# Moving SBUF-only products and casts to GpSimd, and pairing the fifth q tiles, in a fused linear-attention and gated feed-forward kernel

## The chip, the cores and the metric

The kernel runs on one core of a Trainium2 chip. Five engines work side by side: TensorE (PE; its weight loads are listed as PEld), VectorE (DVE), ScalarE (ACT), GpSimd (POOL) and SyncE (SP, which issues most of the DMAs). The metric is the device time of one execution in microseconds; less is better.

## The reference

Linear attention with cosine weighting for 8 batches of 8 heads, 576 tokens and 64 features, and behind it a feed-forward layer over all 4608 tokens:

```python
def phi(x, c, s):                       # c, s: cos and sin of (pi/2) * pos / S
    r = np.maximum(x, 0.0)
    return np.concatenate([r * c, r * s], axis=-1)
q_p, k_p = phi(q, cos_w, sin_w), phi(k, cos_w, sin_w)
kv = np.einsum('bhsf,bhsd->bhfd', k_p, v)
z = np.sum(k_p, axis=2)
num = np.einsum('bhsf,bhfd->bhsd', q_p, kv)
den = np.einsum('bhsf,bhf->bhs', q_p, z)[..., None] + 1e-06
x = (num / den)                         # to (4608, 512)
h = x @ w_in                            # 512 -> 2048
g = h * np.cos(h)
out = g @ w_out                         # 2048 -> 512
```

## The kernel before, in words

**Tiles of tokens.** A batch has 576 tokens: four tiles of 128 and 64 tokens left over, which form a fifth tile that is half full. A batch's tokens lie in two interleaved halves of the partitions: `load` brings five tiles of one half's 64 partitions (every second one) and four tiles of the other's; which half has five depends on whether the batch is even or odd. The fifth tiles of two batches together make one tile of 128 tokens, so there are nine chunks of 512 tokens for the feed-forward layer: chunks 0 to 7 are the batches' four full tiles, and chunk 8 gathers the four paired fifth tiles.

**Attention of a batch** (`first_attention`, `second_attention`, `attention`). `prep` (L364 on ACT, L365 on DVE) applies ReLU and the cosine or sine weight to a 128x512 tile of k or q, SBUF to SBUF, fp32 to fp16. `cast_v` (L378 ACT, L379 DVE) casts v to fp16; only for batches 0 and 1 may it also be put on POOL, and the order in use puts none there. `kv` (L391) makes the k-v products. A q tile is transposed either by PE (`q_pe`, L420, with a copy out of PSUM) or by DMA (`q_dma`, L428, on SP's queue). `num` (L450) multiplies the transposed q tile by the k-v products; DVE divides (L474, L476); `x_pe` (L496) or `x_dma` (L504) transposes the result into `xT` or, for fifth tiles, `xR`.

**A fifth q tile before the change.** The q tile of each batch is prepared and transposed on its own, with zeros in the half of the partitions that belongs to the other batch (the memsets at L962 clear them once); it goes to `qT4_0` or `qT4_1`. For an odd batch `num` then sums two products per head, the earlier batch's and its own. For batch 0 a function of its own, `late_q0`, does this with PE during layer 1 of chunk 0.

**Layer 1 of a chunk** (`layer1`). For chunks 0 and 1 blocks of two columns by 256 tokens (L542). From chunk 2 on a column block is either plain (`layer1_plain`, L582: four matmuls of 512 columns, then a gate), or four blocks together are done by a seven-product scheme (`layer1_fast`, L685: 28 matmuls of 256 columns). `FAST1` says how many of a chunk's four groups are of the second kind; chunk 2 has none. The scheme needs sums of weights (`w_in_sums`, into `WS`), sums of the tokens' tile (`layer1_sums`, into `XS`), and copies and additions out of PSUM into `Z3` (L318, L319, L698).

**Gates.** `gate` is h * cos(h) of one PSUM bank: ACT makes the cosine (L514, into `ch`), DVE multiplies (L519; one operand in PSUM, the other in SBUF). In a seven-product group half of the results lie in SBUF (`uz`); `out2` makes one cosine over 1024 elements (L707) and one product of 1024 elements with both operands in SBUF. This product, like all of `sums`, is a DVE instruction at L323. A page line `L323 ... gT<-Z,ch` is such a product; `S<-gT`, `gT<-gT`, `XS<-xT`, `WS<-w_in_sb` and `T<-w_out_sb` are the fp16 sums.

**Layer 2** (`layer2_plain` for chunk 0, L784; else `layer2`, L849) is done by the same seven-product scheme over the whole chunk, with DVE sums of the gated values ahead of it, and its results go by L318, L319 and L863 into `ost` and by DMA (L745) to the output.

**The order.** All instructions are first put down as steps (`Plan.add`) with their possible engines. A long table `KEYS` gives for each step its place (the number divided by ten, in hundredths of a microsecond of the plan's own time) and, as its last digit, which of the possible engines takes it (0 where there is only one). The steps are then issued in the order of their places, so each engine's queue has a fixed order; synchronization is by what the steps read and write. Chunk c's layer 1 overlaps layer 2 of chunk c-1 and the attention of the batches behind it.

Of the kernel before, what the change touches and what calls it, by code (L numbers as in the profile page):

```python
# [12 lines left out]
F32 = mybir.dt.float32  # L13
# [180 lines left out]
def kernel(  # L194
# [9 lines left out]
    nc = tc.nc  # L204
    B, H, S, D = q.shape
    Dm, Dff = moe_w_in.shape
    P = 128
# [886 lines left out]
```

## Time and profile before

| | |
|---|---|
| time, median of 3 runs | 281.59 us (280.68 to 282.78) |
| the profiled execution | 280.85 us, of it 279.0 us from the first to the last instruction |
| granted TensorE clock | 0.999 |
| busy PE / PEld / DVE / ACT / POOL | 269.2 / 217.3 / 251.4 / 218.9 / 8.3 us |
| the DVE products with both operands in SBUF, 128x1024 | 20, of some 1.22 us |
| preps on ACT / DVE | 104 of some 0.73 us / 56 of some 0.48 us |
| v casts on ACT / DVE / POOL | 20 / 18 / 0 |

All durations are of one execution, the profiled one. Busy time is the time in which an engine has at least one instruction under way; instructions of one engine overlap by some hundredths of a microsecond, so that preps of 0.48 us start every 0.40 us. PE's matmuls overlap far more: a row's mean is the time until a matmul's last result, and the spacing of matmuls is what adds up.

### The profile page before, as it was taken

How to read it: one execution, taken by the hardware profiler on the slowest of the kernel's cores; microseconds unless marked ns; L12 is line 12 of the kernel's file. 1: busy time of each engine (PE TensorE's matmuls, PEld its weight loads, DVE VectorE, ACT ScalarE, POOL GpSimd, SP SyncE). 2: the span in 40 equal slices, each digit the busy share in tenths (PEclk: the TensorE clock that was granted, in tenths of full speed). 3: DMA queues.
4: the chain of work that ended last, by engine and by line, in shares of the span. 5: the costliest groups of instructions: out<-in, count | busy, mean ns of one | idle time of the engine just before them, and what ended most of it. 6: DMA issues, size and time to landing. Idle time of an engine off the chain costs nothing.

```text
span 279.0 us, 6853 instructions
## 1 busy us (share of the span) xinstructions
PE 269.2 (96%) x2715; PEld 217.3 (78%) x2715; DVE 251.4 (90%) x449; ACT 218.9 (78%) x401; POOL 8.3 (3%) x21
## 2 busy tenths in 40 slices
PE   7779999999999999999999999999999999999994
PEld 2458767678766677789879887998788888888883
DVE  2977798999999999999999999999999999998872
ACT  2856698899999999999999999984684686777210
POOL 1430020000000000000000000000000000000000
PEclk9999999999999999999999999999999999999999
DMA  6999999999999999999999999737210400200324
GB/s 208 315 201 232 281 312 282 309 218 172 328 269 253 210 288 247 310 235 230 245 264 195 346 277 265 154 58 205 39 39 4 188 2 0 78 0 2 151 78 150
DMA packets 77599, 53.30 MB, mean 191 GB/s; under 512 B 46080, under 2 KB 75264, under 8 KB 77568
## 3 DMA queue, kind: packets, MB, share of 16 engines
q1 hardware_dynamic: 72608, 48.12, 67.7%
q0 software_dynamic: 4224, 4.19, 9.3%
q10 hardware_dynamic: 736, 0.57, 0.6%
q8 instruction: 21, 0.34, 0.5%
q14 instruction: 10, 0.08, 0.1%
HBM read 36.74 MB, written 9.44 MB: 166 GB/s over the span
## 4 chain that ended last, share of the span: by engine, by line
PE 85%; DMA 5%; ACT 4%; DVE 3%; issue 2%; ACTq 0%
PE M L849 33%; PE M L685 15%; PE M L542 8%; PE M L582 7%; PE TR L685 6%; PE M L784 4%; PE ATT L450 3%; DMA qT<-KQ 3%; PE ATT L391 3%; DMA qm<-in_q_dram 2%; ACT KQ L364 2%; PE TR L582 1%; ACT ch L514 1%; PE M L420 1%; DVE KQ L365 1%
## 5 line engine op out<-in xcount | busy, mean ns | idle before, releaser
L514 ACT ACTIVATE ch<-M 128x512 f32<-128x512 f32 x90 | 53.9, 603 | 14.0 <-PE M L685 6.8
L849 PEld LDWEIGHTS <-gT 128*128 128x128 f16 x560 | 54.1, 98 | 8.2
L519 DVE TENSOR_TENSOR gT<-M,ch 128x512 f16<-128x512 f32 x84 | 55.9, 685 | 4.5 <-ACT ch L514 4.0
L849 PE MATMUL M<-w_out_sb,gT 128*128 128x256 f16 x448 | 56.4, 273 | 0.0
L364 ACT ACTIVATE KQ<-km,CS 128x512 f16<-128x512 f32 x56 | 38.9, 732 | 0.5 <-DMA km<-in_k_dram 0.5
L364 ACT ACTIVATE KQ<-qm,CS 128x512 f16<-128x512 f32 x48 | 33.5, 728 | 4.4 <-DMA qm<-in_q_dram 4.2
L685 PEld LDWEIGHTS <-w_in_sb 128*128 128x128 f16 x320 | 31.0, 98 | 4.6 <-issue 0.2
L849 PE MATMUL M<-T,S 128*128 128x256 f16 x256 | 31.5, 273 | 0.0
L318 ACT ACTIVATE ost<-M 128x512 f32<-128x512 f32 x32 | 19.2, 600 | 15.0 <-PE M L849 9.5
L542 PE MATMUL M<-xT,w_in_sb 128*128 128x256 f16 x256 | 30.1, 272 | 0.6 <-DVE gT L519 0.5
L542 PEld LDWEIGHTS <-w_in_sb 128*128 128x128 f16 x256 | 24.6, 98 | 4.8 <-issue 1.2
L582 PE MATMUL M<-xT,w_in_sb 128*128 128x512 f16 x112 | 27.9, 379 | 0.0
L849 PEld LDWEIGHTS <-S 128*128 128x128 f16 x256 | 24.9, 98 | 3.4
L476 DVE TENSOR_TENSOR x<-ATT,rec 128x512 f16<-128x512 f32 x32 | 22.1, 692 | 2.5
L685 PEld LDWEIGHTS <-WS 128*128 128x128 f16 x216 | 20.6, 98 | 2.6
L582 PEld LDWEIGHTS <-w_in_sb 128*128 128x128 f16 x128 | 11.9, 98 | 9.2
L365 DVE TENSOR_SCALAR KQ<-qm,CS 128x512 f16<-128x512 f32 x32 | 14.2, 479 | 4.8 <-DMA qm<-in_q_dram 4.8
L450 PEld LDWEIGHTS <-qT 128*128 128x128 f16 x320 | 14.7, 98 | 4.4 <-issue 1.4
L323 DVE TENSOR_TENSOR S<-gT 128x2048 f16<-128x2048 f16 (+1 forms) x16 | 17.2, 1083 | 0.0
L450 PE MATMUL ATT<-kvz,qT 128*128 128x65 f16 x288 | 15.3, 194 | 0.9 <-DVE kvz L406 0.4
L323 DVE TENSOR_TENSOR gT<-Z,ch 128x1024 f16<-128x1024 f32 x13 | 15.9, 1219 | 0.3
L698 DVE TENSOR_TENSOR Z<-M,Z 128x512 f32<-128x512 f32 x22 | 14.9, 686 | 0.9 <-PE M L685 0.5
(138 smaller groups left out, 448.6 us busy)
## 6 DMA issues: line engine op xcount, KB each, us to landing
out_dram<-ost SPq DMA_DIRECT2D x33, 256.0 KB, 2.7
qm<-in_q_dram SPq DMA_DIRECT2D x8, 640.0 KB, 5.7
km<-in_k_dram SPq DMA_DIRECT2D x8, 640.0 KB, 6.5
qm<-in_q_dram SPq DMA_DIRECT2D x8, 512.0 KB, 6.0
km<-in_k_dram SPq DMA_DIRECT2D x8, 512.0 KB, 6.5
vm<-in_v_dram SPq DMA_DIRECT2D x6, 640.0 KB, 6.8
vm<-in_v_dram SPq DMA_DIRECT2D x6, 512.0 KB, 6.6
w_in_sb<-in_moe_w_in_dram POOLq DMA_DIRECT2D x4, 512.0 KB, 8.6
```

Source lines behind the costliest of these rows:

```text
L318: "ACT": lambda: nc.scalar.activation(out=out_, in_=in_, func=AF.Copy),
L323: return lambda: q.tensor_tensor(out=out_, in0=in0, in1=in1, op=op)
L364: fn = {"ACT": lambda: nc.scalar.activation(out=out_, in_=in_, func=AF.Relu, scale=sc), "DVE": lambda: nc.vector.tensor_scalar(out=out_, i ...
L365: "DVE": lambda: nc.vector.tensor_scalar(out=out_, in0=in_, scalar1=0.0, scalar2=sc, op0=ALU.max, op1=ALU.mult)}
L450: nc.tensor.matmul(bank[hb][:, hh * D1:(hh + 1) * D1], lhsT=a[:, h, :], rhs=z[:, h, :], start=(i == 0), stop=(i == len(parts) - 1))
L476: nc.vector.tensor_tensor(out=split(x16[n][:, hs, :], k), in0=A[:, :, :, 0:D], in1=split(rec[n][:, hs], k).unsqueeze(3).broadcast_to((P, k ...
L514: act(0.5, due, lambda: nc.scalar.activation(out=ch[c], in_=bank, func=AF.Sin, bias=math.pi / 2.0, scale=1.0), [key], [("ch", c)])
L519: dve(0.61, due, lambda: nc.vector.tensor_tensor(out=dst, in0=a, in1=b, op=ALU.mult), [key, ("ch", c), *rd], dkeys)
L542: nc.tensor.matmul(M1[m][:, jj * 2 * P:(jj + 1) * 2 * P], lhsT=w_in_sb[:, cc, j * P:(j + 1) * P], rhs=X[:, cc, ts], start=(jj == 0 and cc ...
L582: nc.tensor.matmul(M, lhsT=w_in_sb[:, cc, j * P:(j + 1) * P], rhs=X[:, cc, :], start=(cc == 0), stop=(cc == NCT - 1))
L685: nc.tensor.matmul(bank[0][:, j * TH:(j + 1) * TH], lhsT=a(cc, j), rhs=b[:, cc, :], start=(first and j == 0 and cc == 0), stop=(last and j ...
L849: nc.tensor.matmul(bank[0][:, tt * MH:(tt + 1) * MH], lhsT=a[:, j, tt * P:(tt + 1) * P], rhs=b[:, j, :], start=(first and (apart or tt == ...
```

## The change

- `sums` gets an option for POOL, and `out2` uses it: the 1024-element product may go to POOL. `cast_v` may go to POOL for every batch. The order table is new throughout. By its digits, 17 of the 21 products and 21 of the 38 v casts are on POOL; the rest of the work is also divided anew between ACT and DVE.
- Chunk 2 has one seven-product group instead of four plain column blocks; its weight sums come before layer 1 of chunk 2.
- The fifth q tiles of two batches are prepared and transposed together, when the odd batch's turn comes: both batches' loads leave their rows in the two halves of one raw tile. `CS` gets a column with both batches' weights. `late_q0` and the memset of q are gone, `qT4` is one buffer. `num` takes for the fifth tile every second column of `qT4` (64 columns) against one batch's k-v products, and writes 64 rows of PSUM for each batch. The stores of chunk 8 read 64 neighbouring partitions instead of every second one.

```diff
 KEYS = (
...
 )
-    cs_np = np.zeros((P, 2, 2, NT + 1), dtype=np.float32)
+    cs_np = np.zeros((P, 2, 2, NT + 2), dtype=np.float32)
...
-            cs_np[n::2, n, g, :] = w[:S5].reshape(R, NT + 1)
+            cs_np[n::2, n, g, :NT + 1] = w[:S5].reshape(R, NT + 1)
+            cs_np[n::2, :, g, NT + 1] = w[NT:S5:NT + 1, None]
...
-    qT4 = [sb(f"qT4_{n}", [P, H, P]) for n in range(2)]
+    qT4 = sb("qT4", [P, H, P])
...
-    VCAST, VCAST_01 = ("DVE", "ACT"), ("DVE", "ACT", "POOL")
+    VCAST = ("DVE", "ACT", "POOL")
...
-    def sums(due, n, out_, in0, in1, op, rd, wr, lazy=None, rate=0.523e-3):
+    def sums(due, n, out_, in0, in1, op, rd, wr, lazy=None, rate=0.523e-3, pool=None):
         def go(q):
             return lambda: q.tensor_tensor(out=out_, in0=in0, in1=in1, op=op)
-        either(due, {"DVE": 0.07 + n * rate, }, {"DVE": go(nc.vector)}, rd, wr,
-               lazy=lazy)
+        cost = {"DVE": 0.07 + n * rate}
+        if pool:
+            cost["POOL"] = pool
+        either(due, cost, {"DVE": go(nc.vector), "POOL": go(nc.gpsimd)}, rd, wr, lazy=lazy, port=False, hint=1)
...
-        sc = CS[:, b % 2, g, t:t + 1]
+        sc = CS[:, b % 2, g, t + (nm == "q" and t == NT):][:, 0:1]
...
-        either(due, {e: cost[e] for e in (VCAST if b > 1 else VCAST_01)}, fn, rd, wr)
+        either(due, {e: cost[e] for e in VCAST}, fn, rd, wr, port=False)
...
-        parts = [(qdst(b, t)[0], kvz[b % 2])]
+        a = qdst(b, t)[0]
         rd = [qdst(b, t)[1]] + [("kvz", b % 2, i) for i in range(2)]
         if t == NT:
-            parts.insert(0, (qT4[1 - b % 2], kvz[1 - b % 2]))
-            rd += [("qT4", 1 - b % 2)] + [("kvz", 1 - b % 2, i) for i in range(2)]
+            rd += [("kvz", 1 - b % 2, i) for i in range(2)]
...
-                for i, (a, z) in enumerate(parts):
+                for n2 in range(2) if t == NT else [None]:
+                    rows_, cols, z = (slice(0, P), slice(0, P), kvz[b % 2]) if n2 is None else (
+                        slice(n2 * R, (n2 + 1) * R), slice(n2, P, 2), kvz[n2])
                     nc.tensor.matmul(
-                        bank[hb][:, hh * D1:(hh + 1) * D1], lhsT=a[:, h, :], rhs=z[:, h, :],
-                        start=(i == 0), stop=(i == len(parts) - 1))
+                        bank[hb][rows_, hh * D1:(hh + 1) * D1], lhsT=a[:, h, cols], rhs=z[:, h, :],
+                        start=True, stop=True)
...
-    FAST1 = {3: 3, 4: 3, 5: 3, 6: 3, 7: 4, 8: 4}
+    FAST1 = {2: 1, 3: 3, 4: 3, 5: 3, 6: 3, 7: 4, 8: 4}
...
-                 rate=1.045e-3)
+                 rate=1.045e-3, pool=2.6)
...
-        for i, nm in enumerate("qkv"):
+        for i, nm in enumerate("kv"):
...
-        for t in range(NT + 1):
+        for t in range(NT + b % 2):
             due = T + 8 + 1.2 * t
...
-    def late_q0():
-        for g in range(2):
-            prep(0, "q", NT, g, "DVE", 24, after=[("g", 0, 0, 0)])
-        q_pe(0, NT, TR, ("TR", 0), "ACT", 25)
-
     first_attention()
     layer1(0)
-    late_q0()
```

More of the change, by code (lines that the diff above doesn't have):

```diff
@@ L237, in sb @@
         return pool.tile(shape, dt, name=name)
-    CS = sb("CS", [P, 2, 2, NT + 1], F32)
+    CS = sb("CS", [P, 2, 2, NT + 2], F32)
     IDENT = sb("IDENT", [P, P])
@@ L411, in qdst @@
     def qdst(b, t):
-        return (qT[t], ("qT", t)) if t < NT else (qT4[b % 2], ("qT4", b % 2))
+        return (qT[t], ("qT", t)) if t < NT else (qT4, "qT4")
     def q_pe(b, t, bank, key, eng, due):
@@ L448, in mm @@
                 h = hb * HB + hh
-                for i, (a, z) in enumerate(parts):
+                for n2 in range(2) if t == NT else [None]:
+                    rows_, cols, z = (slice(0, P), slice(0, P), kvz[b % 2]) if n2 is None else (
+                        slice(n2 * R, (n2 + 1) * R), slice(n2, P, 2), kvz[n2])
                     nc.tensor.matmul(
-                        bank[hb][:, hh * D1:(hh + 1) * D1], lhsT=a[:, h, :], rhs=z[:, h, :],
-                        start=(i == 0), stop=(i == len(parts) - 1))
+                        bank[hb][rows_, hh * D1:(hh + 1) * D1], lhsT=a[:, h, cols], rhs=z[:, h, :],
+                        start=True, stop=True)
         full.update((key, False) for key in keys)
         for hb in range(2):
-            pe(HB * len(parts), MMA, due, lambda hb=hb: mm(hb), rd, [keys[hb]])
+            pe(HB * (1 + (t == NT)), MMA, due, lambda hb=hb: mm(hb), rd, [keys[hb]])
         if pair is None:
@@ L761, in store @@
             dst = out.rearrange("(i n s) m -> n i s m", n=2, s=S)[n][2 * h + i0:2 * h + 2, 0:S5, f]
-            put(due, dst.rearrange("i (p t) m -> p t i m", t=NT + 1)[:, NT], blocks(O, n)[:, i0:, f],
+            put(due, dst.rearrange("i (p t) m -> p t i m", t=NT + 1)[:, NT], O[n * R:(n + 1) * R, i0:, f],
                 keys, *((nc.scalar, "ACT") if n else (nc.sync, "SP")), nb=kb / (1 + i0))
@@ L767, in store_tile @@
             dst = out.rearrange("(i n s) m -> n i s m", n=2, s=S)[n][2 + i, 0:S5, 0:MH]
-            put(due, dst.rearrange("(p t) m -> p t m", t=NT + 1)[:, NT], blocks(ost[o], n)[:, i, 0:MH],
+            put(due, dst.rearrange("(p t) m -> p t m", t=NT + 1)[:, NT], ost[o][n * R:(n + 1) * R, i, 0:MH],
                 [("ost", o, 0, i)], *((nc.scalar, "ACT") if n else (nc.sync, "SP")), nb=65.5)
```

241 rows, old and new, of the table KEYS are left out of this document.

## The prediction

> **What bounds the kernel now.** I read the busy shares first, then the same shares by stretch, then the chain that ended last, and last the single instructions of the engines that the change touches.
>
> Busy time per engine, the chain by line (both from the page), and the stretches from 80 us on:
>
> ```profile
> PE 269.2 (96%) x2715; PEld 217.3 (78%) x2715; DVE 251.4 (90%) x449; ACT 218.9 (78%) x401; POOL 8.3 (3%) x21
> ...
> PE 85%; DMA 5%; ACT 4%; DVE 3%; issue 2%; ACTq 0%
> ```
>
> ```profile
> 80.00:107.00 27.00, 26.76 (x294) 19.80 (x291) 25.85 (x46) 26.46 (x52) 0.00 (x0) 1.00 1.14 232
> 107.00:134.00 27.00, 26.80 (x293) 22.60 (x292) 26.12 (x46) 26.44 (x51) 0.00 (x0) 1.00 1.07 263
> 134.00:161.00 27.00, 26.93 (x292) 22.38 (x291) 26.16 (x47) 26.91 (x51) 0.00 (x0) 1.00 1.17 268
> 161.00:188.00 27.00, 27.00 (x292) 22.90 (x290) 26.46 (x46) 25.28 (x46) 0.00 (x0) 1.00 0.85 187
> ```
>
> The columns are start:end, length, then busy us (and count) of PE, PEld, DVE, ACT and POOL, the granted clock, the DMA share and GB/s. TensorE (PE) is full from 80 us on. Two engines run close behind it: VectorE (DVE) is idle only 0.5 to 1.2 us of 27, ScalarE (ACT) as little until 161 us. GpSimd (POOL) does nothing there. So work taken off DVE or ACT shortens nothing by itself; only less PE work does, or fewer gaps in PE. But a DVE that gets more than about 1 us late per stretch is the bound at once.
>
> **The change part by part, PE first.** Two edits take PE work away. A group of chunk 2 goes from four plain column blocks (16 matmuls of 512 columns) to seven products (28 of 256 columns). In the chain, in order of time, both kinds stand by themselves:
>
> ```profile
> 108.70 0.86 PE TR L582 x4
> ...
> 124.28 0.44 PE TR L685 x4
> ```
>
> So 4 x 0.86 = 3.44 us become 7 x 0.44 = 3.08 us: -0.36. Second, the fifth q tile of batch 0 is no longer transposed on its own (`late_q0`). Eight transposes take 0.61 us with the last one's latency; sixteen take 1.06, so one more costs (1.06 - 0.61) / 8 = 0.056 us and the eight 0.45 us:
>
> ```profile
> 27.26 0.61 PE L420 MATMUL TR<-IDENT,KQ 128*128 128x128 f16 x8
> ...
> 39.97 1.06 PE L420 MATMUL M<-IDENT,KQ 128*128 128x128 f16 x16
> ```
>
> PE is on the path there too (it fills 24.25 us of the 25 between 20 and 45), so **PE's saving is 0.36 + 0.45 = 0.81 us**. The products that end the fifth tile (L450) stay 16 per pair of batches; each now gives 64 rows instead of 128. Bounds: no row has such a shape; 16 of them cost 0.5 us of PE per pair, so four pairs can lose or gain at most about 1 us if the time halves or goes up by half. I take 0, since the row's spacing goes with the 65 columns, which stay.
>
> **Fifth tiles elsewhere.** Per even batch, two preps and one transpose go: eight preps (0.73 us each on ACT, 0.48 on DVE), three DMA transposes from SP's queue, for batch 0 the copy out of PSUM (1.0 us on ACT), and one memset of 0.49 us on DVE ahead of the first load. That memset ended at 1.42 us and the second q load was issued at 1.54, right behind the first (0.73 + 0.75), so it held the load by nothing: 0. The rest is off PE: 0 on the path while ACT and DVE keep up. `qT4` becomes one buffer; its users are a batch pair apart (some 54 us), so no new wait. The last stores read 64 neighbouring partitions instead of every second one; they land 1.9 to 2.5 us after issue now, and I take no change.
>
> **What moves to GpSimd.** I count in the order table of the diff (per planned step a place in time, and as last digit the engine chosen). Of the SBUF-only products 17 of now 21 are on POOL; of the v casts 21 of 38, 11 of them 128x1024, three 128x512, seven 128x256. DVE gets rid of 16 products and nine casts and takes over in exchange six preps, net five copies out of PSUM, and the sums of chunk 2's new group. ACT loses 14 preps and 12 casts. With the rows' durations:
> - DVE: -16 x 1.22 (products) - 4.3 (casts) + 6 x 0.48 (preps) + 5 x 0.69 (copies) + 1.7 (four sums of 0.42) + 0.7 (other) = about -15 us.
> - ACT: -14 x 0.73 - 10.3 (casts) + 1.1 (chunk 2) = about -19 us.
> - POOL: a product there has no row. The nearest: a memset of 512 elements on POOL takes 0.52 us and one of a single element 0.10, so 0.83 ns per element and stream, 0.95 us for 1024. A product reads two tiles and writes one: between one stream (0.95) and three in turn (2.75 us). I take 2.3, toward the upper end because three tiles move. A cast of 1024 lies between 0.95 and 1.8; I take 1.1. The sum is 17 x 2.3 + 11 x 1.1 + 4.7 (the smaller casts) = 56 us of POOL, 20% of the span, so POOL itself is no bound.
>
> [...]
>
> The results of POOL are read late: the sums of the next chunk's layer 2 follow mostly 4 us or more behind. The tightest is the last group of the last chunk: its product is placed 3.8 us ahead of the sums that read it. So a product up to 3.8 us is hidden.
>
> **What DVE pays for POOL's company.** This decides. The trace has one place of each kind with POOL at work, its DMA issue at 36.7 to 38.2 us and at 11.1 to 14.4:
>
> ```profile
> 36.71 1.48 POOL L942 DMA_DIRECT2D w_out_sb<-in_moe_w_out_dram  x2 [0.30 <-POOL w_out_sb L954]
> ...
> 37.08 0.60 DVE L365 TENSOR_SCALAR KQ<-km,CS 128x512 f16<-128x512 f32 x1
> 37.60 0.67 DVE L519 TENSOR_TENSOR gT<-M,ch 128x512 f16<-128x512 f32 x1
> ```
>
> ```profile
> 11.09 3.34 POOL L928 DMA_DIRECT2D w_in_sb<-in_moe_w_in_dram  x4 [0.30 <-POOL w_in_sb L922]
> ...
> 12.56 0.67 DVE L379 CAST V<-vm 128x256 f16<-128x256 f32 x2
> 13.15 1.52 DVE L365 TENSOR_SCALAR KQ<-km,CS 128x512 f16<-128x512 f32 x2
> ```
>
> And two preps with POOL idle:
>
> ```profile
> 121.94 0.88 DVE L365 TENSOR_SCALAR KQ<-qm,CS 128x512 f16<-128x512 f32 x2
> ```
>
> The gate at 37.60, which reads one operand from PSUM, is not stretched (0.67; its mean is 0.685). SBUF-to-SBUF preps and casts are: two preps take 1.52 instead of 0.88, one 0.60 instead of 0.48, and the casts 0.67 instead of the usual 0.48 (0.20 from start to start, and 0.28). That is 0.95 us over four or five stretched instructions, **0.2 us each**. What is not in the trace: one of DVE's sums (L323, f16, both operands in SBUF) beside a POOL product that reads SBUF. It is a TENSOR_TENSOR like the unharmed gate, and SBUF to SBUF like the stretched preps. Bounds for a sum that meets a product: 0, and all that is left of the product. By the order table DVE has a sum inside the 2.3 us of ten products, with 1.3 us left on average, and eight preps, casts or sums inside a v cast after 60 us, 0.6 us each: 0 to 18 us of DVE time in all. I take 0.2 us each, the mean stretch that rows show: 18 x 0.2 = 3.6 us, at most five meetings (1.0 us) in one 27 us stretch, and DVE has about that idle there or has it freed. In 134:161, where the table frees only 0.1 us, 1.0 stands against 0.84 idle: +0.2 on the path.
>
> **Sum**: 280.85 (the profiled execution; span 279.0 and 1.85 around it) - 0.81 + 0.2 = 280.2. The median of the runs is 0.74 above the profiled one, so **280.9 us** as a median, 0.2% less than 281.59. What a measurement here can tell from no change is about 1%, 278.8 to 284.4.
>
> **Rivals.**
> *B, GpSimd holds DVE's sums for the rest of its instruction.* For it: the sums run at two elements per ns (2048 in 1.22 us), like the preps a fast SBUF form, and the prep of 37.08 ended (37.68) only after the first of POOL's two issues had (37.45). Against it: the stretches were 0.3 us each at most, and a TENSOR_TENSOR was not touched. Working: the waits by stretch, from 80 us on in steps of 27, are 2.2, 2.9, 4.3, 2.7, 3.0 and 1.0 us. What the order table frees on DVE there is 0, 2.1, 0.1, 1.4, 2.8 and 3.8. Waits above what is freed: 2.2 + 0.8 + 4.2 + 1.3 + 0.2 = 8.7; with DVE's idle time used up first (1.15, 0.88, 0.84, 0.54, 0.70, 0.84) 1.0 + 0 + 3.4 + 0.8 = 5.2. Gates queue behind a held sum on DVE, PSUM banks stay full, and PE waits. So +5.2 to +8.7 less 0.81: 286.0 to 289.5, middle 287.7. It decides from about 11 us of waits on.
>
> This is also what the Trainium skill says (SBUF — State Buffer, Who interferes with whom): a VectorE instruction with two SBUF inputs contends with a GpSimd instruction that reads SBUF, and the loser is blocked for the whole instruction. The trace agrees for the preps and for the gate; for sums nothing here shows it.
>
> *C, POOL's own queue is late.* The second and third parts of w_in are now issued behind three v casts on POOL (12.0 and 12.9 us before, some 14.3 and 15.2 now), and layer 1 of chunk 0 needs them from 24 and 27.7 us. Before, the parts landed every 3 us up to 26.4. If the casts hold them by more than 1.5 us, PE waits 1 to 2 us: 282.5.
>
> *D, the relief also closes PE's gaps.* PE idles 1.3 us between 20 and 161 us (0.66, 0.10, 0.24, 0.20, 0.07 by stretch), and the casts spread over three engines start the first k-v products some 0.7 us earlier. All of it: 281.59 - 0.81 - 1.3 - 0.7 = 278.8. For it: ACT and DVE get room. Against it: those gaps are single waits for a DMA transpose or a bank, which the change does not touch.
>
> *That it does nothing* is nearly the forecast: DVE and ACT were covered by PE before.
>
> **How the numbers follow.** Forecast 0.47 (279.8 to 282.5), B 0.38, C 0.07, D 0.08. D gives 0.05 of faster by over 1%, and I add 0.01 for a chunk-2 group that gains more. B is slower by over 1% nearly always; with a little of C that is 0.40. The rest is within 1%: 0.54. The range runs from D's 278.8 to 288.5, which leaves a quarter of B outside.
>
> **What would show it.** Right: PE busy about 0.8 us less, L323's 128x2048 sums still near 1.22 us beside POOL products of 2 to 2.6 us, DVE 236 to 241 us. B: those sums at 2 us and more, DVE busy near 250, ACT and PE waiting for DVE gates between 80 and 190 us. C: PE idle at 24 to 28 us before L542. Wrong altogether: POOL products over 3.8 us, so that layer 2 of the last chunk waits for POOL.

## The result, and the profile after

The changed kernel takes 300.44 us (median of four runs, 299.21 to 301.32) against 281.80 us for the kernel before in the same session: ratio 1.067, interval 1.062 to 1.072. It is 18.6 us slower. The profiled execution took 299.86 us, of it 298.1 us of span. Below, us are worked out from ratios with 280.5 us for the kernel before; 1% is 2.8 us.

The page after, the busy shares and the chain that ended last:

```profile
PE 273.9 (92%) x2719; PEld 217.4 (73%) x2719; DVE 258.7 (87%) x444; ACT 204.1 (68%) x365; POOL 71.3 (24%) x59
...
PE 42%; DVE 13%; ACT 4%; issue 3%; DMA 1%; DVEq 0%; ACTq 0%
```

This chain reaches back only to 104.67 us, so its shares add up to 63% of the span, those of before to 99%. Of what each chain covers, PE fell from 85 of 99 to 42 of 63, about two thirds, and DVE rose from 3 of 99 to 13 of 63, a fifth. DVE got rid of much work and is still busier (251.4 before). The windows of 27 us that the prediction showed, in the same columns (PE, PEld, DVE, ACT, POOL, clock, DMA share, GB/s):

```profile
80.00:107.00 27.00, 23.98 (x225) 15.19 (x223) 25.01 (x41) 21.51 (x42) 6.54 (x5) 0.94 1.09 211
107.00:134.00 27.00, 24.19 (x271) 19.37 (x268) 26.49 (x46) 24.44 (x46) 5.01 (x3) 1.00 1.12 251
134.00:161.00 27.00, 26.93 (x265) 21.89 (x263) 25.11 (x45) 22.53 (x40) 8.78 (x5) 1.00 1.06 239
161.00:188.00 27.00, 23.29 (x244) 18.68 (x242) 26.05 (x40) 18.33 (x35) 8.39 (x5) 1.00 0.81 196
```

PE was busy for 26.76 to 27.00 of the 27 us in each of them before; in three of the four it now has 23.29 to 24.19. The clock of 0.94 in the first one does not explain it: run 15 below has 1.00 there, and PE has 24.71. Which DVE instructions became longer is seen in the groups with shapes kept apart (line, out<-in, count, busy us, mean ns):

```profile
L522 DVE TENSOR_TENSOR gT<-M,ch 128x512 f16<-128x512 f32 x82 | 54.8, 683 | 8.6 <-ACT ch L517 8.4
...
L323 DVE TENSOR_TENSOR gT<-gT,S 128x2048 f16<-128x2048 f16 x6 | 11.2, 1872 | 0.0
...
L323 DVE TENSOR_TENSOR gT<-gT 128x2048 f16<-128x2048 f16 x6 | 9.3, 1556 | 0.0
...
L323 DVE TENSOR_TENSOR WS<-w_in_sb,WS 128x512 f16<-128x512 f16 x3 | 3.4, 1138 | 0.0
```

One of these sums before:

```profile
L323 DVE TENSOR_TENSOR gT<-gT,S 128x2048 f16<-128x2048 f16 x6 | 7.3, 1218 | 0.0
```

The gate (L522, one operand in PSUM) is as it was: 683 ns against 685. The three sums, with both operands in SBUF, had means of 1218, 1216 and 418 ns before. One hold in the timeline (start, us, engine, line; in brackets the idle time before):

```profile
87.69 2.35 POOL L323 TENSOR_TENSOR gT<-Z,ch 128x1024 f16<-128x1024 f32 x1 [6.16 <-ACT ch L710]
87.97 3.15 DVE L323 TENSOR_TENSOR gT<-gT,S 128x2048 f16<-128x2048 f16 x1
...
91.34 0.69 DVE L479 TENSOR_TENSOR x<-ATT,rec 128x512 f16<-128x512 f32 x1
...
92.18 0.42 PE L453 MATMUL ATT<-kvz,qT 128*128 128x65 f16 x8 [1.82 <-DVE x L479]
```

POOL's product runs from 87.69 to 90.04. A sum of 1.22 us begins on DVE inside it and takes 3.15. The division behind it (L479) starts late, its PSUM bank stays full, and PE stands still for 1.82 us. I compared every DVE instruction's duration with the median of its form before; what it lasts longer is called its stretch. It is 1.1 us in the whole trace before, 21.9 us after. 15 sums lost 18.0 us of it, 14 preps and casts 3.9.

POOL's own instructions, by shape:

```profile
L323 POOL TENSOR_TENSOR gT<-Z,ch 128x1024 f16<-128x1024 f32 x10 | 24.6, 2463 | 66.0 <-ACT ch L710 66.0
L382 POOL CAST V<-vm 128x1024 f16<-128x1024 f32 x11 | 15.7, 1445 | 59.2 <-DMA vm<-in_v_dram 19.9 <-PE TR L585 19.5 <-ACT KQ L366 14.3
```

### The profile page after: what moved, and what is told of

Same layout as the page of the kernel before. It is cut to its first block, busy times and chain, and to the rows that moved or that the text cites. A ratio compares the mean times of both kernels' runs of the same rounds, so it can differ in the third digit from the quotient of the medians.

```text
span 298.1 us, 6907 instructions
## 1 busy us (share of the span) xinstructions
PE 273.9 (92%) x2719; PEld 217.4 (73%) x2719; DVE 258.7 (87%) x444; ACT 204.1 (68%) x365; POOL 71.3 (24%) x59
## 4 chain that ended last, share of the span: by engine, by line
PE 42%; DVE 13%; ACT 4%; issue 3%; DMA 1%; DVEq 0%; ACTq 0%
PE M L852 22%; PE M L688 10%; PE TR L688 5%; DVE gT L323 3%; PE M L585 3%; DVE gT L522 2%; DVE S L323 2%; ACT ch L517 2%; PE ATT L453 1%; ACT KQ L366 1%; DMA qT<-KQ 1%; DVE qT L323 1%; DVE Z L701 1%; PE TR L585 1%; ACT M L318 1%
## 5 line engine op out<-in xcount | busy, mean ns | idle before, releaser
L517 ACT ACTIVATE ch<-M 128x512 f32<-128x512 f32 x88 | 51.3, 596 | 21.6 <-PE M L585 6.4
L522 DVE TENSOR_TENSOR gT<-M,ch 128x512 f16<-128x512 f32 x82 | 54.8, 683 | 8.6 <-ACT ch L517 8.4
L688 PEld LDWEIGHTS <-w_in_sb 128*128 128x128 f16 x336 | 32.4, 97 | 12.5 <-issue 7.4
L382 POOL CAST V<-vm 128x1024 f16<-128x1024 f32 (+2 forms) x21 | 21.2, 1028 | 81.6 <-DMA vm<-in_v_dram 22.8
L323 POOL TENSOR_TENSOR gT<-Z,ch 128x1024 f16<-128x1024 f32 x10 | 24.6, 2463 | 66.0 <-ACT ch L710 66.0
L366 ACT ACTIVATE KQ<-km,CS 128x512 f16<-128x512 f32 x47 | 32.0, 714 | 2.1 <-DMA km<-in_k_dram 2.1
L366 ACT ACTIVATE KQ<-qm,CS 128x512 f16<-128x512 f32 x43 | 29.8, 719 | 4.4 <-DMA qm<-in_q_dram 4.3
L318 ACT ACTIVATE ost<-M 128x512 f32<-128x512 f32 x31 | 18.3, 597 | 17.7 <-PE M L852 10.9
L545 PEld LDWEIGHTS <-w_in_sb 128*128 128x128 f16 x256 | 24.6, 98 | 4.9 <-issue 1.3
L585 PE MATMUL M<-xT,w_in_sb 128*128 128x512 f16 x96 | 25.7, 398 | 0.3 <-DVE gT L522 0.2
L479 DVE TENSOR_TENSOR x<-ATT,rec 128x512 f16<-128x512 f32 x32 | 22.1, 691 | 2.3
L453 PEld LDWEIGHTS <-qT 128*128 128x128 f16 (+1 forms) x320 | 13.7, 101 | 8.2 <-issue 6.6
L710 ACT ACTIVATE ch<-Z 128x1024 f32<-128x1024 f32 x15 | 15.8, 1053 | 4.1 <-DVE Z L701 4.0
L367 DVE TENSOR_SCALAR KQ<-km,CS 128x512 f16<-128x512 f32 x33 | 16.9, 543 | 1.1 <-DMA km<-in_k_dram 1.1
```

What stands on the lines that cost most here:

```text
L318: "ACT": lambda: nc.scalar.activation(out=out_, in_=in_, func=AF.Copy),
L323: return lambda: q.tensor_tensor(out=out_, in0=in0, in1=in1, op=op)
L366: fn = {"ACT": lambda: nc.scalar.activation(out=out_, in_=in_, func=AF.Relu, scale=sc), "DVE": lambda: nc.vector.tensor_scalar(out=out_, i ...
L367: "DVE": lambda: nc.vector.tensor_scalar(out=out_, in0=in_, scalar1=0.0, scalar2=sc, op0=ALU.max, op1=ALU.mult)}
L382: "POOL": lambda: nc.gpsimd.tensor_copy(out=out_, in_=in_)}
L479: nc.vector.tensor_tensor(out=split(x16[n][:, hs, :], k), in0=A[:, :, :, 0:D], in1=split(rec[n][:, hs], k).unsqueeze(3).broadcast_to((P, k ...
```

## The experiments

The theory after the result was the forecast's rival B: a POOL instruction that reads SBUF holds a DVE instruction with two SBUF operands until it ends, and PE pays for most of that (hold theory). The main rival: the new order itself is slow, and POOL has little to do with it (order theory). A third: a product takes 2.4 us on POOL instead of 1.2, so that its result comes late and its buffers come free late (late theory).

**1 to 3. The work taken back off POOL.** In the changed kernel, products back to DVE (1), casts back to ACT (2), both (3):

```diff
# in all three: where the table's digit names an engine that is gone, the last one left
-            e = list(s["opts"])[i - 1]
+            e = list(s["opts"])[min(i, len(s["opts"])) - 1]
# 1 and 3
-                 rate=1.045e-3, pool=2.6)
+                 rate=1.045e-3)
# 2 and 3
-    VCAST = ("DVE", "ACT", "POOL")
+    VCAST = ("DVE", "ACT")
```

> The changed kernel with its 17 products back on DVE at the same places of the order; the 21 casts stay on POOL. Hold theory (a POOL instruction that reads SBUF holds DVE's SBUF-only instructions until it ends): in the changed kernel's trace 15.6 us of DVE's stretch end with a product and 5.7 us with a cast, so about 15 us of the 18.7 go: 284 to 288 us, with only sums and preps beside casts stretched. Order theory (the new order and division of work loses the time, whatever POOL does): within 3 us of 300. Late theory (the product's result comes 1.2 us later from POOL and its buffers are held longer): also about 285, but with the sums beside casts unstretched.

> The changed kernel with the 21 casts that POOL had now on ACT, at the same places; the products stay on POOL. Hold theory: only the 5.7 us that end with a cast go, and part of that comes back as ACT work (about 14 us spread over 240 us, where ACT is idle 94 us): 294 to 297 us. Order theory: about 300. Late theory: about 300, since the products stay.

> Both of the foregoing: no product and no cast on POOL, everything else of the change kept (order, pairing, chunk 2's group). Hold theory: no DVE instruction is stretched after 40 us and the time falls to 280 to 286 us (DVE gets 18 us of products back, about what it had before). Order theory: over 293 us.

Measured: 295.13 us (ratio 1.049, 1.046 to 1.052), 301.87 us (1.075, 1.073 to 1.078) and 300.39 us (1.069, 1.068 to 1.071). The stretch of DVE's instructions went to 6.8, 15.1 and 0.7 us. So the holds go with POOL's work, but of the time only 1.8% (5 us) comes back, in run 1. All three lie above what the hold theory expected, and runs 2 and 3 fit the order theory. I do not take them as decisive: the new order has no places on DVE and ACT for the work (17 products of 1.22 us, 21 casts), and in these in-order queues it may cost as much as the holds. That is argued, not tried. The next run keeps the order of before.

**4. Only the products moved, in the order of before.**

```diff
-        either(due, {"DVE": 0.07 + n * rate, }, {"DVE": go(nc.vector)}, rd, wr,
+        either(due, {e: 0.07 + n * rate, }, {e: go(nc.vector if e == "DVE" else nc.gpsimd)}, rd, wr,
...
-                 rate=1.045e-3)
+                 rate=1.045e-3, e="POOL")
```

> The kernel before with its 20 products on POOL instead of DVE, order and all else as before. Hold theory: the products of 2.36 us cover 47 us of some 175, in which about 11 to 14 sums start: 14 to 18 us of stretch, which the 20 x 1.14 us that DVE gets rid of make good at most in part: 288 to 300 us. Order theory: 280 to 283 us, since the order is the old one.

Measured: 293.91 us, ratio 1.047 (1.043 to 1.050). Two windows of this kernel, in the columns above:

```profile
80.00:107.00 27.00, 27.00 (x304) 20.40 (x303) 26.28 (x47) 26.63 (x53) 0.00 (x0) 1.00 1.18 235
...
134.00:161.00 27.00, 24.35 (x262) 19.34 (x260) 24.63 (x37) 24.18 (x45) 5.73 (x3) 1.00 1.00 226
```

The first window has nothing on POOL, and PE is full. In the second, with three products on POOL, PE has 24.35 us against 26.93 before, although DVE has more idle time (24.63 busy against 26.16). 11 of the 20 products met a sum, for 18.6 us of stretch behind 40 us; the loss is 13.2 us. DVE is rid of 20 x 1.22 = 24.4 us and the kernel is slower. But not all of the loss is holds. A product on POOL ends some 1.1 us later than on DVE, and ACT and DVE wait for its end in 12 places, 12.1 us in all; in the kernel before they never wait for POOL. The largest group (line, waited for, us in total, times, longest):

```profile
ACT Z L318 <- POOL gT L323: 5.8, 7, 1.5
```

These are copies into a buffer `Z` that the product still reads. So in the old order holds and late products both cost time, and this run does not part them. In the changed kernel such waits are 4.2 us in 6 places, and its chain holds no product of POOL, but six sums of 1.50 to 2.71 us that are held.

**5. POOL only writes.** In the changed kernel POOL's products and casts become memsets of the same tiles, so it is busy about as long (64.2 us) and reads nothing; this part of the computation is left out.

```diff
-        either(due, cost, {"DVE": go(nc.vector), "POOL": go(nc.gpsimd)}, rd, wr, lazy=lazy, port=False, hint=1)
+        either(due, cost, {"DVE": go(nc.vector),
+            "POOL": lambda: [nc.gpsimd.memset(w, 0.01) for w in writes]}, rd, wr, lazy=lazy, port=False, hint=1)
...
-              "POOL": lambda: nc.gpsimd.tensor_copy(out=out_, in_=in_)}
+              "POOL": lambda: [nc.gpsimd.memset(w, 0.01) for w in (raw["v"][:, hs, t:t + nt, 0:4], out_)]}
...
-                 rate=1.045e-3, pool=2.6)
+                 rate=1.045e-3, pool=2.6, writes=(cc2, g4, U))
```

> The changed kernel, same order and same engines, but each POOL product is replaced by three POOL memsets of the tiles that it read and wrote (about 0.95 + 0.95 + 0.5 = 2.4 us, the same waits ahead and behind), and each v cast on POOL by a memset of its output and of four columns of its input. POOL is thus as busy at the same places but reads no SBUF; these parts of the computation are left out. Hold theory, by reading: no sum of DVE is stretched, only preps and casts may still be; 279 to 283 us, so that the whole loss of the change is gone with the order kept. Order theory: 295 to 300 us. Late theory (POOL's long occupancy and late results): 295 to 300 us.

Measured: 287.39 us, ratio 1.023 (1.020 to 1.026). No sum is stretched, only preps and casts by 5.7 us. It is POOL's reading, not its being busy, that holds the sums. But I had expected 279 to 283 us, and 2.3% stay, so the holds of the sums are not the whole loss.

**6. Side by side.** A small kernel by itself, not the kernel's computation: VectorE runs short series of one form (six, or three of the 2048-element sum), alone and with one POOL instruction begun with them.

```python
for p in ("none", "product", "cast", "memset"):
    for d in dve:
        v.memset((M if p == "memset" else A)[:, 0:1], 0.25)   # starts both together
        gp[p]()
        for _ in range(3 if d == "sum2048" else 6):
            dve[d]()
```

> Not the kernel at all, only the disputed pair measured by itself: beside no POOL instruction, a POOL product of 1024 fp32, a POOL cast of 1024 and a POOL memset of 1024, DVE does a row of sums of 512 and of 2048 (fp16, two SBUF operands), products of 512 fp32 (two SBUF operands), gates (one operand in PSUM), preps, and copies from PSUM. Hold theory: beside the product one sum of 512 takes about 2.4 us instead of 0.42, one of 2048 ends 1.1 us after POOL does, the fp32 product is held too, gates and PSUM copies keep 0.69; beside the memset the sums keep 0.42 and 1.22 if only reading counts, the preps are held. Theory of the forecast: no instruction more than 0.3 us longer.

Its timeline, the last five of a series (L34 sum of 512, L37 gate, L38 prep), first alone, then beside a product, a cast and a memset of 1024 elements on POOL:

```profile
10.41 2.27 DVE L34 TENSOR_TENSOR S<-U,W 128x512 f16<-128x512 f16 x5
...
21.34 3.59 DVE L37 TENSOR_TENSOR H<-PS,C 128x512 f16<-128x512 f32 x5
...
25.38 2.57 DVE L38 TENSOR_SCALAR K<-C,SC 128x512 f16<-128x512 f32 x5
...
32.56 4.28 DVE L34 TENSOR_TENSOR S<-U,W 128x512 f16<-128x512 f16 x5
...
49.55 3.59 DVE L37 TENSOR_TENSOR H<-PS,C 128x512 f16<-128x512 f32 x5
...
53.58 4.53 DVE L38 TENSOR_SCALAR K<-C,SC 128x512 f16<-128x512 f32 x5
...
62.73 2.98 DVE L34 TENSOR_TENSOR S<-U,W 128x512 f16<-128x512 f16 x5
...
79.83 3.23 DVE L38 TENSOR_SCALAR K<-C,SC 128x512 f16<-128x512 f32 x5
...
87.68 2.27 DVE L34 TENSOR_TENSOR S<-U,W 128x512 f16<-128x512 f16 x5
...
102.64 3.22 DVE L38 TENSOR_SCALAR K<-C,SC 128x512 f16<-128x512 f32 x5
```

A product on POOL (2.35 us) costs the sums 4.28 - 2.27 = 2.01 us and the preps 1.96; a cast (1.04 us) costs 0.71 and 0.66; a memset costs the sums nothing and the preps 0.65. The gate is 3.59 in every company, and so is a copy out of PSUM. One series meets one POOL instruction, so what is lost is the rest of that instruction, once.

The Trainium skill (SBUF — State Buffer, Who interferes with whom) states this rule: two SBUF operands on VectorE contend with a GpSimd instruction that reads SBUF, not with one that only writes, and the loser waits for the whole instruction. The rows of the sums agree: 2.01 us more beside the product, 0.71 beside the cast, none beside the memset. The preps have one operand in SBUF and are held by the memset too, so this rule, put in this way, does not cover them, and the prediction's word that the trace agrees for the preps goes too far.

**7. Only the pairing.** The kernel before with the fifth q tiles paired; `late_q0`'s steps and the others that fall away are struck from the old order.

```diff
+GONE = (0, 138, 139, 140, 141, 338, 339, 340, 649, 650, 651, 966, 967, 968)
+KEYS = [k for n, k in enumerate(KEYS) if n not in GONE]
# and the change's own edits of CS, qT4, prep, qdst, num and the two stores
```

> The kernel before with the fifth q tiles paired and nothing else of the change; the steps that fall away are dropped from the old order. All theories of the loss: not slower. PE loses 0.45 us of transposes on its path: 279.8 to 281, a ratio of 0.996 to 1.000.

Measured: 280.45 us, ratio 1.000 (0.999 to 1.001). PE is rid of the eight transposes at 27.26 us and begins its next matmuls at the same moment, 27.99 us (27.96 before):

```profile
27.99 2.23 PE L548 MATMUL M<-xT,w_in_sb 128*128 128x256 f16 x19 [0.54 <-DVE gT L525]
```

Before:

```profile
27.96 2.23 PE L542 MATMUL M<-xT,w_in_sb 128*128 128x256 f16 x19
```

The matmuls wait for a bank that a gate empties. The transposes had stood in the place of that wait.

**8. The freed time filled again.** Run 4 with two DVE memsets of 512 fp16 elements behind each product on POOL.

```diff
+            if e == "POOL":
+                return lambda: (q.tensor_tensor(out=out_, in0=in0, in1=in1, op=op), nc.vector.memset(JUNK, 0.0), nc.vector.memset(JUNK, 0.0))
```

> The kernel before with its 20 products on POOL, as in the earlier run that took 293.9 us, but DVE gets two memsets of 512 fp16 (about 1.1 us) in the place of each product, so that nothing is freed on DVE. If DVE's freed time was set off against the holds (as the rival of the prediction counted it): 20 x 1.1 us more work, 305 us or more. If a hold costs PE its length and the freed time buys nothing: 293 to 298 us.

Measured: 294.61 us, ratio 1.051 (1.048 to 1.055). That is 0.7 us above run 4 by the medians and 1.3 us by the ratios, and the intervals overlap. The 40 memsets took 10.9 us (272 ns each), so less than half of the 24.4 us that were freed. Even so: of 10.9 us more DVE work some 1 us is seen. Time freed on DVE is worth little here.

**9. The new order with nearly nothing on POOL.** The changed kernel, POOL's products and, from batch 1 on, its casts cut to memsets of one column; this part of the computation is left out.

```diff
+            "POOL": lambda: [nc.gpsimd.memset(w, 0.01) for w in writes]}, rd, wr, lazy=lazy, port=False, hint=1)
...
+              "POOL": (lambda: [nc.gpsimd.memset(w, 0.01) for w in (raw["v"][:, h0, t, 0:1], V1[:, t, h0, 0:1])])
+              if b else lambda: nc.gpsimd.tensor_copy(out=out_, in_=in_)}
...
+                 rate=1.045e-3, pool=2.6, writes=(cc2[:, 0:1], g4[:, 0, 0, 0:1], U[:, 0:1]))
```

> The changed kernel, same order and engines, but what POOL had is cut to memsets of one column of the same tiles (waits and order kept): the 17 products, and the v casts of batches 1 to 7, are left out of the computation; batch 0's casts stay. POOL is then free in the steady state, and ACT and DVE have what the new order leaves them. Hold theory: the new order runs to its plan, no DVE instruction is stretched after 40 us, 279 to 282 us. Order theory (something in the new order, the pairing or the group of chunk 2 costs time by itself): 284 us or more, as in the run with POOL only writing (287.4 us), whose last 7 us the hold theory puts down to preps held by memsets.

Measured: 285.17 us, ratio 1.018 (1.014 to 1.023), with no stretch on DVE behind 42 us. I had expected no loss. The new order itself costs some 5 us. Run 5 speaks to the late theory: POOL is busy about as long there as in the changed kernel, ACT still waits 2.4 us for it (4.2 in the changed kernel), and yet run 5 lies only 0.5% (1.3 us, uncertain by some 1.5) above this one. So late results explain little of the change's loss. The waits of run 9 between 66 and 160 us, in the columns of run 4 (the profiled execution, of 287.53 us, is the longest of the four):

```profile
ACT KQ L367 <- DMA km<-in_k_dram: 3.3, 3, 1.6
...
ACT KQ L367 <- DMA qm<-in_q_dram: 2.2, 3, 1.5
...
PEld L456 <- DMA qT<-KQ: 1.3, 1, 1.3
DVE KQ L368 <- DMA qm<-in_q_dram: 1.2, 1, 1.2
```

In the same view of the kernel before no prep waits for a load. And in the chain of run 9, from 84 us on:

```profile
86.52 2.92 SPq L433
...
89.49 7.35 DMA qm<-in_q_dram
...
96.92 0.07 ACT KQ L367
```

The second load of q is issued behind 2.92 us of DMA transposes (L433) in SP's queue and lands 7.35 us later; the prep waits for it.

**10. Only products that met nothing.** Run 4 with nine of the products on POOL, those that met no sum there.

```diff
+    FREE = ((3, 0), (3, 2), (6, 0), (6, 1), (7, 1), (7, 3), (8, 1), (8, 2), (8, 3))
...
+                 rate=1.045e-3, e="POOL" if (c, g) in FREE else "DVE")
```

> The kernel before with only those 9 of its 20 products on POOL beside which no DVE instruction was stretched in the run with all 20 there. Hold theory: no stretch, so no loss: 279.5 to 281.5 us; and since PE is the bound no gain either, although DVE gets rid of 9 x 1.14 = 10 us. Theory that a product on POOL costs by its lateness (2.4 instead of 1.2 us): 9/20 of the 13.3 us that the run with all 20 lost, about 286 us.

Measured: 284.72 us, ratio 1.015 (1.012 to 1.018). Two of the nine met a sum after all; one of them:

```profile
132.85 2.35 POOL L323 TENSOR_TENSOR gT<-Z,ch 128x1024 f16<-128x1024 f32 x1 [19.27 <-ACT ch L708]
132.97 2.53 DVE L323 TENSOR_TENSOR XS<-xT 128x512 f16<-128x512 f16 x1
```

These two lost 2.11 and 2.08 us, 4.2 in all, and the kernel is 4.2 us slower by its ratio. That the figures are equal does not show the cause: I had expected no loss, and the late theory's 286 us is nearly as close. Behind the product shown PE waits for ACT's copy into `Z`, and the copy waits for POOL, not for the held sum:

```profile
135.24 0.60 ACT L318 ACTIVATE Z<-M 128x512 f32<-128x512 f32 x1 [0.76 <-POOL gT L323]
...
135.89 0.38 PE L686 MATMUL M<-xT,WS 128*128 128x256 f16 x2 [0.71 <-ACT Z L318]
```

So this run does not tell a hold from a late product. It does show that choosing products by an old trace does not keep them clear: with 11 products back on DVE the times shift.

**11 and 12. Products alone, casts alone.** Run 9 with the products complete (11), and with the casts complete (12).

```diff
# 11
+            "POOL": go(nc.gpsimd)}, rd, wr, lazy=lazy, port=False, hint=1)
# 12
+              "POOL": lambda: nc.gpsimd.tensor_copy(out=out_, in_=in_)}
```

> As the run with one-column memsets, but the 17 products are real again; only the v casts of batches 1 to 7 are left out. Hold theory: the products' holds alone, 13 to 16 us above that run: 293 to 297 us. Order theory: no more than the run with one-column memsets.

> As the run with one-column memsets, but all v casts on POOL are real again; the 17 products are left out. Hold theory: the casts' holds alone, 4 to 6 us above that run: 283 to 287 us, and with the products' part about the 300.4 us of the change.

Measured: 295.64 us (1.053, 1.049 to 1.057; stretch 17.5 us) and 287.69 us (1.026, 1.021 to 1.031; stretch 6.6). Over run 9 the products cost 3.4% or 9.6 us, the casts 0.75% or 2.1 us. Both are less than I had expected (13 to 16 and 4 to 6 us), and the intervals of runs 9 and 12 overlap, so the casts' part is barely clear of noise.

**13 to 15. Half the bytes of the loads.** Run 9 (13), the kernel before (14) and the changed kernel (15) with shorter loads of q, k and v from batch 2 on; for the tokens that are not loaded the kernel goes on with what the buffers held.

```diff
+        k5, k4 = (NT + 1, NT) if b < 2 else (2, 2)
-                nc.sync.dma_start(out=blocks(m, n)[:, h], in_=five)
+                nc.sync.dma_start(out=blocks(m, n)[:, h, 0:k5, :], in_=five[:, :, 0:k5, :])
-                nc.sync.dma_start(out=blocks(m, 1 - n)[:, h, 0:NT, :], in_=four)
+                nc.sync.dma_start(out=blocks(m, 1 - n)[:, h, 0:k4, :], in_=four[:, :, 0:k4, :])
```

> The new order with GpSimd's products and casts from batch 1 on cut to memsets of one column, as in the run before it (285.2 us, 1.018), and now also with the loads of q, k and v from batch 2 on cut to two of five and two of four tokens per partition, so that about half their bytes are left; those numbers of the output are not the reference's. Transfer theory: in the new order the preps wait for loads that land late (ScalarE's and VectorE's preps wait 6.4 us for loads of q and k between 66 and 160 us, TensorE 2.3 us for a transposed q; before 0.0 and 1.4), because the 16 DMA engines are full there and each raw buffer is loaded again only after its last prep. With half the bytes the loads land early: 279.5 to 281.5 us, ratio 0.997 to 1.004, and those waits go. Order theory: the new order is short of slack in ScalarE's and VectorE's own queues, and the loads only show it: 283.5 to 285.5, ratio 1.012 to 1.019.

> The kernel before with the same cut in the loads of q, k and v from batch 2 on; nothing else changed. It is the control. Both theories: TensorE is full and no prep waits for a load between 66 and 160 us, so 279.5 to 280.8 us, ratio 0.997 to 1.002. If it gains more than 0.5%, the transfers cost time in the kernel before too, and the run of the new order is to be read against this one.

> The changed kernel, GpSimd's products and casts complete, with the same cut in the loads of q, k and v from batch 2 on. Transfer theory: the new order's own 5 us go and the holds stay, 300.4 less 3 to 5: 295 to 297 us, ratio 1.053 to 1.06. If holds and late loads feed each other, more goes: below 294. Order theory: nothing goes, 299 to 301, ratio 1.066 to 1.072.

Measured: 282.33 us (1.005, 1.003 to 1.007), 280.42 us (0.999, 0.997 to 1.001) and 296.70 us (1.057, 1.053 to 1.062). In run 13 no prep and no matmul waits for a load or a transpose between 66 and 160 us. So the transfers cost 1.2% (3.4 us) of the new order's 1.8%, beyond the control; in the complete change about 0.8% (2.2 us). The transfer theory had 1.004 as its upper end for run 13: 0.6%, some 1.8 us, of the order's cost is something else and stays open. Why the loads come late was read from one chain and not tried by itself.

**The account.** The whole is 6.7%. By runs 9, 11 and 12: the order 1.8, the products 3.4, the casts 0.75, together 6.0. The rest of 0.6 may be what they do to each other, but each of these differences is itself uncertain by some 0.6. With the transfers eased (15 against 13) POOL's work costs 5.2%, 14.7 us. Run 5 lies only some 1.3 us above run 9, with late results and held preps both in it, so most of POOL's part is holds.

## Why the prediction was wrong, point by point

- **The step that failed: "0.2 us each" for DVE's meetings with POOL.** The mechanism was in the prediction, its price was not. The step averaged stretches beside POOL's DMA issues. In the changed kernel 29 stretched instructions lost 21.9 us, 20.8 us more than before and not 3.6, nearly all of it beside a product or a cast; run 6 has 2.01 us for one meeting with a product. The step's own upper bound, all that is left of POOL's instruction, gave 18. Of the two ends it took the wrong one: the row of 37.08, a prep that ended only behind POOL's first issue, was the sign. All four preps that are stretched in the trace before end 0.23 to 0.25 us behind the end of such an issue. The issues last only 0.74 to 0.94 us, so little was left of them: 0.2 us was a matter of their length and no price for a product of 2.35 us.
- **Rival B had the right mechanism, and 287.7 was still too little.** Its 16.1 us of meetings between 80 and 242 us were near: 14.5 us of stretch lie there in the changed kernel. But it set off the DVE time that the change frees or that was idle, and was left with 5.2 to 8.7. Run 8 shows that freed time covers little (10.9 us of DVE work put back cost some 1 us), and POOL's work cost 14.7 us in run 15 over run 13. My reading, which no run tries by itself, is that a hold delays the gates behind it at once, and time freed in another place does not reach it. B also had nothing for the new order.
- **Not in the sum at all: the new order's transfers.** It priced what left PE, DVE and ACT, but not where the loads and transposes now stand in SP's queue, in windows where the DMA share was already 1.07 to 1.17. That is 3.4 us with POOL's work left out and 2.2 us in the complete change; 1.8 us more is open.
- **A product hidden for up to 3.8 us: only in part.** The prediction asked who reads the result, but not who waits for the buffers that the product reads. In the changed kernel ACT waits 4.2 us for them, though not in the chain.
- **-0.45 us for `late_q0`: wrong.** PE was busy nearly throughout there, but without the transposes its next matmuls waited for a bank; run 7 gained nothing. The -0.36 of chunk 2 was not tried alone.
- **Right:** DVE's relief of 15 us (258.7 less 21.9 of stretch is 236.8; 251.4 less 1.1 before is 250.3, so 13.5); nothing for the products of 64 rows (64 of them took 2.2 us, 0.55 for 16, where 0.5 was taken); a POOL product at 2.3 us (2.36 where it meets nothing) and a cast at 1.1 (1.05); gates unharmed. The Trainium skill (GPSIMD Engine Reference, 3.1) has 4497 ns on GpSimd for a `tensor_tensor` add of 2048 fp32 elements; half of it, an estimate of 2.25 us for 1024, is near the 2.36 of the product as well. Three streams in turn are 3 x 0.85 + 0.10 = 2.65 us by the prediction's own rate, not 2.75; the 2.3 does not hang on it. ACT's relief was 14.8 us, not 19. POOL's new work is 63 us, not 56, since POOL is held too.
- **Rivals C and D:** in layer 1 of chunk 0 nothing waits for w_in (C), and PE's gaps grew (D).

## What to carry to other kernels

Where an in-order engine runs close to full beside a full TensorE, price a move by the worst single delay it can put into that queue, not by the busy time it takes off; here time freed elsewhere hardly paid a delay back. In run 6, moving work to GpSimd left VectorE's instructions with an operand in PSUM alone and cost those with SBUF operands only the rest of GpSimd's instruction. A slower instruction also gives its buffers back later: ask who waits for them. A new order moves the loads too: look where they stand in the DMA-issuing queue whenever the transfers are near their limit.

## What the runs showed of the hardware that was not expected

- A held sum does its own work only after POOL's instruction: in the changed kernel's trace it ended 0.28 us (512 elements), 0.55 us (1024) or 1.08 us (2048) after POOL's end. So what it loses depends on when it starts and not on its size.
- POOL is held in turn: the product, 2.35 us alone, took 3.35 us in the series of 2048-element sums, and a cast 2.07 instead of 1.04. In the changed kernel the casts of 1024 elements average 1445 ns, the products 2463.
- A memset on POOL, which reads nothing, holds preps (five took 3.22 us instead of 2.57) but no sum.
